# Five edits to a one-core backward kernel: product shapes, weight transposes, gradient stores, small matmul widths, early weight chunks

## The chip, the cores and the metric

The kernel is written for one core of a Trainium2 chip. That core has a matrix engine (PE, with a weight load PEld in front of each matmul), a vector engine (DVE), an activation engine (ACT), GpSimd (POOL) and a queue engine (SP). Each of them carries out its own instructions strictly in their written order. DMAs are issued by SP, ACT and POOL. The metric is the device time of one execution in microseconds (us), lower is better.

## What is computed

The reference is one gated block and its gradients. With L = 2048, D = 576, N = 128 and F = 4608:

```
xn  = layernorm(x)
s   = causal_conv(xn, K) + xn * Dskip                   # K from A, B, C, dt: D x L
g   = silu( (silu(xn @ w1) * (xn @ w3)) @ w2 )
out = x + s * g
returns out and the gradients of x, A_re, A_im, B_re, B_im, C_re, C_im,
        log_dt, Dskip, w1, w3, w2
```

All matmul inputs are bf16. The convolution is done by blocks of 512 with transforms written as matmuls. The gradients of A, B, C and log_dt need, for each of the 576 channels, sums over time of a gradient times powers of the rates; the kernel gets them as products of two small factors ("q" over 64 steps, "pz" over 32), in 36 chunks of 16 channels.

## The kernel before

The program is unrolled in Python, and a planner orders it: `self.at(us)` sets a planned time as the priority of what is written next, and the planner turns the priorities, the data dependences and its own estimates into one fixed order for every engine and queue. Buffers come from pools; a tile that is asked for again waits for its last user. Planned times and times of the trace are not the same: T0 = 560 of `backward` corresponds to about 800 us in the trace, T2 = 1208 to about 1610 us.

The stages, in order of time in the trace:

- **Prologue (0 to 150).** Layer norm, selectors, spectra of the input.
- **Hidden layer beside the convolution kernel (150 to 530).** `ffn_hidden` makes gate and up for every 512 of F; pairs of row tiles go to DRAM (`GI_dram`, L728, from POOL; `gu_t` has three buffers) and the product to `H_dram` (L727, from SP). `kgen_chunk` makes q and pz for the 36 chunks; `pz` is stored in three planes (minus cosine, cosine, sine; the first is made by POOL in L477).
- **`forward_tail` (530 to 800).** w2 is loaded in nine chunks of 4 x 128 rows (`w2g`, L769, from POOL), then the second layer, the convolution and the gradient of the gate branch; `go_o` is transposed by PE (L833) into `goT`.
- **`ssm_bwd_conv` and 18 groups of 256 columns of F (800 to 1605).** A group (`phase6_group`) makes the hidden gradient (`ph`, L1226), copies it (`gh`, L1229, ACT), multiplies it into `gu` and `gg` (L1232, DVE), stores both to `GU_dram` and `GG_dram` in halves (L1239, from SP), and makes the weight gradients (L1254, L1273, L1279, L1281). ACT evicts each of these and issues the DMA that stores it (L1259, L1276, L1285, L1286). `load_w2T` brings the group's w2 rows (two POOL loads, two transposing DMAs on SP), and `gates` prepares the next group from two loads of `GI_dram` on POOL (L1193, L1194).
- **`param_chunk` (19 chunks from about 1300 on, 17 in the last stage).** SP loads `gz`, `qT` (a transposing DMA) and `pz`. For each half of a chunk PE makes two PSUM tiles of 8 channels x 2 x 32 (`et_ps`, L989; the pool has three buffers). DVE multiplies each with two planes of pz (four instructions, L996, into `pr_q`) and sums (two, L998). Five `final_block`s turn the sums into gradients: DVE works in two scratch tiles `f0` and `f1` (L1029), ACT copies results out of them (L1050) and after each copy issues the DMA that stores it (L1051).
- **`phase6_inputs` (1605 to the end).** For 16 row tiles, the gradient of xn: `ggc` and `guc` are transposed from DRAM by SP (two buffers each), and 144 matmuls per tile (L1333) use w1 and w3 transposed. These come in four parts, through `wT_into` (L1131): `wTA` (12 of 36 column blocks, own memory), `wTB` (12), `goT`'s memory (4) and `go_o`'s memory (8). Each part is five transposing DMAs for w1 and five for w3, one for every 128 rows of D (the last has 64).

All DMA transposes are issued by line L1140, on SP.

Of the kernel before, what the change touches and what calls it, by code (L numbers as in the profile page):

```python
# [11 lines left out]
ALU = mybir.AluOpType  # L12
# [4 lines left out]
P = 128  # L17
# [43 lines left out]
class K:  # L61
# [356 lines left out]
    def ssm_kernel(self, T0, TK):  # L418
# [9 lines left out]
        PS = bass.MemoryType.PSUM  # L428
        self.PZ_dram = self.dram.tile([P, NCH, 3, DC, AV], BF16, name="PZ_dram")
        self.Q_dram = self.dram.tile([NCH, P, 2 * DC * BV], BF16, name="Q_dram")  # L430
# [24 lines left out]
    def kgen_chunk(self, ch, E, lhs, mp, sb, qvp, ps, T, TK):  # L455
# [14 lines left out]
        q = qvp.tile([P, DC, 2, BV], BF16, name="q_k")  # L470
        pz = sb.tile([P, 3, DC, AV], BF16, name="pz_k")
        for k, src in ((1, S), (0, C)):
            tt(out=q[:, :, k, :], in0=E[:, 0:QW].rearrange("p (d b) -> p d b", b=BV),
               in1=src[:, 0:QW].rearrange("p (d b) -> p d b", b=BV), op=ALU.mult)
            tt(out=pz[:, 1 + k].rearrange("p d a -> p (d a)"), in0=E[:, QW:], in1=src[:, QW:], op=ALU.mult)
        nc.sync.dma_start(out=self.Q_dram[ch], in_=q[:].rearrange("p d k b -> p (d k b)"))
        nc.gpsimd.tensor_scalar(out=pz[:, 0], in0=pz[:, 2], scalar1=-1.0, scalar2=None, op0=ALU.mult)  # L477
        nc.sync.dma_start(out=self.PZ_dram[:, ch], in_=pz[:])
        v = qvp.tile([P, 2, DC, AV], BF16, name="v_k")
        for k, (Wa, Wb, op) in enumerate(((self.WrT, self.nWiT, ALU.add), (self.nWiT, self.WrT, ALU.subtract))):  # L480
            t = sb.tile([P, DC, AV], BF16, name="t_k")
            for r, W, o in ((1, Wb, t[:]), (0, Wa, v[:, k])):
                tt(out=o.rearrange("p d (a x) -> p d a x", x=4),
                   in0=pz[:, 1 + r].rearrange("p d (a x) -> p d a x", x=4),
                   in1=W[:, ch].rearrange("p h d x -> p (h d) x")[:, :, None, :].to_broadcast([P, DC, AV // 4, 4]),
                   op=ALU.mult)
            tt(out=v[:, k], in0=v[:, k], in1=t[:], op=op)
# [243 lines left out]
    def forward_tail(self, T0, TB, TQ, gctx):  # L731
# [20 lines left out]
        ep = rpool(fw, "o_ep", 2)  # L752
        ep1 = rpool(fw, "o_ep1", 1)
        wpool = rpool(fw, "o_w", 1)
        hp = rpool(fw, "o_h", 2)
# [7 lines left out]
        for t_ in self.goT:  # L763
            nc.gpsimd.memset(t_[rem:P, nfull, :], 0.0)
        w2g = [wpool.tile([P, GRP, D], BF16, name=f"w2g{n}") for n in range(FT // GRP)]
        w2 = [w2g[fi // GRP][:, fi % GRP, :] for fi in range(FT)]
        for n, t_ in enumerate(w2g):
            self.at(T0 - 4 + 2.5 * n)
            nc.gpsimd.dma_start(out=t_[:], in_=aps["B_w2"][n * GRP * P:(n + 1) * GRP * P, :].rearrange(  # L769
                "(c p) d -> p c d", p=P))  # L770
# [46 lines left out]
        for t_ in self.goT[NB // 2:]:  # L817
            nc.gpsimd.memset(t_[rem:P, nfull, :], 0.0)
        self.w2rows = [rowp.tile([P, DT * P], BF16, name=f"w2r{i}") for i in range(4)]
        for w2r in self.w2rows:  # L820
            nc.gpsimd.memset(w2r[:, D:DT * P], 0.0)
        out0 = aps["out_0"].flatten_outer_dims()
        xin = aps["A_u"].flatten_outer_dims()
        for i in range(LT):
# [6 lines left out]
            ptr = tps.tile([P, 1024], BF16, name="ptr")  # L831
            for c, (do, dsz) in enumerate(cfg.dch):
                nc.tensor.transpose(ptr[0:dsz, c * P:(c + 1) * P], go_o[:, i, do:do + dsz], self.ident_bf[:])  # L833
            ts = slice(i % KT * P, (i % KT + 1) * P)
            nc.scalar.copy(out=self.goT[m][:, 0:nfull, ts],
                           in_=ptr[:, 0:nfull * P].rearrange("p (c t) -> p c t", t=P))
            nc.vector.tensor_copy(out=self.goT[m][0:rem, nfull, ts], in_=ptr[0:rem, nfull * P:(nfull + 1) * P])
            self.at(T0 + 44 + TB * i)
# [9 lines left out]
    def ssm_bwd_conv(self, T0, TQ, ps):  # L848
# [3 lines left out]
        with self.tc.tile_pool(name="b_k", bufs=1, side="right") as kp, self.tc.tile_pool(name="b_z", bufs=2, side="right") as zp:  # L852
# [4 lines left out]
            nc.vector.tensor_scalar(out=self.lcol[:], in0=self.lcol[:], scalar1=1.0 / 512, scalar2=None, op0=ALU.mult)  # L857
            self.ones_col = kp.tile([P, 1], BF16, name="ones_col")
            nc.vector.memset(self.ones_col[:], 1.0)
# [3 lines left out]
    def ssm_bwd_params(self, chunk_at, final_at, out, big, S_all, ps):  # L863
# [4 lines left out]
        with self.tc.tile_pool(name="g_k", bufs=1, side="right") as gkp, self.tc.tile_pool(name="g_t", bufs=3, side="right") as tqp, \  # L868
                self.tc.tile_pool(name="g_q", bufs=2, side="right") as qp, \
                self.tc.tile_pool(name="g_r", bufs=1, side="right") as rp:  # L870
            gz = []
            for i in range(2):
# [13 lines left out]
    def conv_bwd_quarter(self, g, kp, zp, ps, T0, TQ):  # L886
# [22 lines left out]
        for b in range(NB):  # L909
# [6 lines left out]
            for tt in range(KT):  # L916
                nc.tensor.matmul(gds[0:1, 0:W], lhsT=self.ones_col[:], rhs=prod[:, tt, :], start=(b == 0 and tt == 0),
                                 stop=(b == NB - 1 and tt == KT - 1))
# [51 lines left out]
    def param_chunk(self, ch, gz, S_all, tqp, qp, rp, ps):  # L970
# [3 lines left out]
        if True:  # L974
# [7 lines left out]
            pz = qp.tile([P, 3, 16, AV], BF16, name="pz")  # L982
            nc.sync.dma_start(out=pz[:], in_=self.PZ_dram[:, ch])
            for h in range(2):
                T = [ps.tile([P, 8, 2, AV], FP32, name="et_ps") for _ in range(2)]
                for dd in range(8):
                    dl = 2 * dd + h
                    for r in range(2):
                        nc.tensor.matmul(T[r][:, dd].rearrange("p k (f t) -> p (k f) t", f=2), lhsT=qT[:, dl, :],  # L989
                                         rhs=gK[:, r, :, :, dl, :].rearrange("p k f t -> p (k f) t"),  # L990
                                         start=True, stop=True)
                d0 = h * (D // 2) + ch * 8
                for s in range(2):
                    pr = rp.tile([P, 2, 8, 2, AV], FP32, name="pr_q")
                    for r in range(2):
                        nc.vector.tensor_tensor(out=pr[:, r], in0=T[r][:], in1=pz[:, s + r, h * 8:h * 8 + 8, :][:, :, None, :]  # L996
                                                .to_broadcast([P, 8, 2, AV]), op=ALU.mult)
                    nc.vector.tensor_reduce(out=S_all[:, 2 * s:2 * s + 2, d0:d0 + 8].rearrange("p k d -> p d k"),  # L998
                                            in_=pr[:].rearrange("p r d k a -> p d k r a"), op=ALU.add, axis=AX.XY)

# [9 lines left out]
    def final_block(self, c, do, dsz, fp, fo, S_all, ps2):  # L1010
# [17 lines left out]
        S2 = ST[v].rearrange("p (r s) n -> p s r n", s=2)[:, 1]  # L1028
        A, B = [fp.tile([P, 4, N], FP32, name=f"f{n}")[v] for n in range(2)]  # L1029
        acc = fp.tile([P, 4], FP32, name="acc")[v]  # L1030
# [48 lines left out]
    def backward(self, T0, TG, TQ, TX, gctx, mats):  # L1079
# [11 lines left out]
        with ExitStack() as out:  # L1091
# [13 lines left out]
            for ai in range(2):  # L1105
                t = wA.tile([P, FA, D], BF16, name=f"wTA{ai}")
                self.wT_into(t[:], ai, 0, wT, lambda c: T2 - 160 + 12 * (2 * c + ai))
            T1 = T0 + 4 * TQ
            N1 = 19
            chunk_at = lambda ch: T1 + 13.5 * ch if ch < N1 else T2 + TX * 1.4 + 13.5 * (ch - N1)  # L1110
            final_at = {20: {0: T2 + 4.5 * TX}, 30: {3: chunk_at(30) + 10}, 33: {1: chunk_at(33) + 10},
# [19 lines left out]
    def wT_into(self, dst, ai, f0, wT, at):  # L1131
        n = dst.shape[1]
        for c, (do, dsz) in enumerate(self.cfg.dch):
            self.at(at(c))
            self.nat_transpose(dst[:, :, do:do + dsz], self.aps[("B_w1", "B_w3")[ai]][do:do + dsz, f0 * P:(f0 + n) * P])
        for f in range(n):
            wT[ai][f0 + f] = dst[:, f, :]
# [6 lines left out]
    def load_w2T(self, gi, T):  # L1144
        nc, cfg = self.nc, self.cfg
        nfl = self.FG // P
        self.at(T)
        w2T = self.wp.tile([P, nfl, cfg.DT, P], BF16, name="w2T")
        for fl in range(nfl):
            fi = gi * nfl + fl  # L1150
            w2r = self.w2rows[fi % len(self.w2rows)]
            nc.gpsimd.dma_start(out=w2r[:, 0:cfg.D], in_=self.aps["B_w2"][fi * P:(fi + 1) * P, :])
            self.nat_transpose(w2T[:, fl], w2r[:])
        return w2T
# [56 lines left out]
    def phase6_group(self, gi, tiles, gwp, ps_h, ps_gw, defer):  # L1211
# [5 lines left out]
        for s in range(LH // 2):  # L1217
# [13 lines left out]
            for t_ in (gu, gg):  # L1231
                nc.vector.tensor_tensor(out=t_[:, sl], in0=gh.rearrange("p j t f -> p (j t) f"), in1=t_[:, sl],  # L1232
                                        op=ALU.mult)
            if s % 2 == 1 and not defer:
                self.phase6_grad2(gi, s // 2, hn, ps_gw, "pgw")
        for (dst, t_) in ((self.GU_dram, gu), (self.GG_dram, gg)):
            for j in range(2):
                ts = slice(j * LH, (j + 1) * LH)
                nc.sync.dma_start(out=dst[ts, :, gi * FG:(gi + 1) * FG].rearrange("t p f -> p t f"), in_=t_[:, ts, :])  # L1239
        self.phase6_grad13(gi, gg, gu, gwp, ps_gw)  # L1240
# [47 lines left out]
    def phase6_inputs(self, T2, TX, FA, wT, late, ps_gw, ps_h, ffps):  # L1288
# [6 lines left out]
        with self.tc.tile_pool(name="x_in", bufs=2) as inp, self.tc.tile_pool(name="x_wB", bufs=1) as wB, \  # L1295
# [10 lines left out]
            def weights(tiles, f0, t):  # L1306
                for ai in range(2):
                    self.wT_into(tiles[ai], ai, f0, wT, lambda c: t)
                return f0 + tiles[0].shape[1]
# [169 lines left out]
```

## Time and profile before

| | us |
|---|---|
| four runs | 2022.34, 2010.83, 2008.61, 2011.96; median 2011.39 |
| the profiled execution (the first of the four) | 2022.34 |
| its span, first to last instruction | 2020.4 |
| PE matmul busy | 1772.6 (88%) |
| PE weight loads | 1297.8 (64%) |
| DVE | 1419.7 (70%) |
| ACT | 1024.2 (51%) |
| POOL | 269.6 (13%) |

The profile's page gives busy time per engine, 40 slices of the span, the DMA queues, the chain of waits that ended last, the costliest groups of instructions and the DMA issues. A group's row reads: line, engine, operation, output <- inputs, shapes, count | busy time, mean ns of one | idle time of the engine just before, and what ended it. The mean granted PE clock over the span is 0.958 of full speed.

### The profile page before, as it was taken

The numbers are of one execution on the slowest core, as the hardware profiler recorded it, in microseconds if no ns is written. First come the engines' busy times: TensorE is split into PE (matmuls) and PEld (weight loads), VectorE is DVE, ScalarE is ACT, GpSimd is POOL, SyncE is SP. The second block draws the span as 40 slices with busy tenths as digits, with TensorE's granted clock in tenths as the row PEclk, the third lists the DMA queues.
The fourth block names the chain that finished last, engine by engine and source line by source line (L and its number), as shares of the span: only waits on it lengthen the run. The fifth ranks groups of instructions, "written<-read, shape, count | busy, mean of one in ns | idle before, by whom it ended". The sixth has DMA issues, their size and how long they took to land. (4 is left out here: it accounts for less than half of the span.)

```text
span 2020.4 us, 41956 instructions
## 1 busy us (share of the span) xinstructions
PE 1772.6 (88%) x17179; PEld 1297.8 (64%) x17179; DVE 1419.7 (70%) x2660; ACT 1024.2 (51%) x1739; POOL 269.6 (13%) x362
## 2 busy tenths in 40 slices
PE   2789999999799988989889998879979967988787
PEld 1444444444478866778777777768768845766666
DVE  7538888888387743495884868758979804398676
ACT  2778888887545554774666656434445201100112
POOL 4003333333321221000000000100000000000000
PEclk9899999999899999999999999989999978999999
DMA  3589888797966688365563555899998999999992
GB/s 85 181 298 320 299 298 297 271 328 274 273 190 157 161 228 222 104 181 159 176 189 115 170 172 151 216 234 235 236 186 212 221 194 186 198 198 196 205 187 56
DMA packets 612907, 417.10 MB, mean 206 GB/s; under 512 B 400395, under 2 KB 558059, under 8 KB 607979
## 3 DMA queue, kind: packets, MB, share of 16 engines
q1 hardware_dynamic: 547200, 280.47, 56.8%
q0 software_dynamic: 24288, 106.94, 15.5%
q10 hardware_dynamic: 41226, 27.02, 5.3%
q8 instruction: 134, 2.20, 0.5%
q14 instruction: 59, 0.48, 0.1%
HBM read 134.06 MB, written 188.01 MB: 159 GB/s over the span
## 5 line engine op out<-in xcount | busy, mean ns | idle before, releaser
L719 PE MATMUL pgu<-wmB_w,xnT 128*128 128x512 bf16 x1152 | 282.4, 380 | 1.2 <-ACT E_k L392 1.2
L1273 PEld LDWEIGHTS <-xn_bf 128*128 128x128 bf16 x2304 | 223.9, 98 | 29.4 <-issue 2.6
L1273 PE MATMUL pgw<-Y,xn_bf 128*128 128x256 bf16 x2048 | 232.3, 273 | 1.6 <-ACT gw L1275 1.6
L996 DVE TENSOR_TENSOR pr_q<-et_ps,pz 128x512 f32<-128x512 f32 x288 | 186.2, 683 | 46.9 <-PE et_ps L989 37.3
L1226 PE MATMUL ph<-w2T,goT 128*128 128x256 bf16 x1440 | 193.3, 283 | 23.3 <-ACT gh L1229 23.2
L719 PEld LDWEIGHTS <-xnT 128*128 128x128 bf16 x1152 | 103.2, 98 | 124.0 <-issue 18.9
L998 DVE TENSOR_REDUCE S_all<-pr_q 128x16 f32<-128x1024 f32 x144 | 175.2, 1216 | 2.2
L1226 PEld LDWEIGHTS <-goT 128*128 128x128 bf16 x1440 | 142.2, 102 | 35.0 <-issue 13.8
L1232 DVE TENSOR_TENSOR Y<-gh,Y 128x1024 bf16<-128x1024 bf16 x128 | 86.3, 682 | 110.8 <-ACT gh L1229 109.3
L785 PE MATMUL po<-w2g,hc 128*128 128x288 bf16 x1152 | 154.1, 292 | 4.2 <-DMA hc<-H_dram 4.2
L1275 ACT CAST gw<-pgw 128x256 bf16<-128x256 f32 x144 | 54.0, 377 | 198.5 <-PE pgw L1273 195.7
L1333 PEld LDWEIGHTS <-ggc 128*128 128x128 bf16 x1152 | 114.8, 101 | 51.8 <-issue 9.5
L1333 PEld LDWEIGHTS <-guc 128*128 128x128 bf16 x1152 | 115.1, 101 | 51.2 <-DMA guc<-GU_dram 18.7
L785 PEld LDWEIGHTS <-hc 128*128 128x128 bf16 x1152 | 113.1, 100 | 34.1 <-DMA hc<-H_dram 4.5
L1373 ACT ACTIVATE X<-X 128x576 f32<-128x576 f32 x16 | 10.9, 683 | 224.0 <-DVE X L1343 205.5
L1254 PE MATMUL pgw<-go_o,X 128*128 128x288 bf16 x896 | 120.2, 288 | 0.0
L722 ACT ACTIVATE s_t<-pgu 128x512 bf16<-128x512 f32 x144 | 87.3, 608 | 52.2 <-PE pgu L721 51.9
L1229 ACT CAST gh<-ph 128x512 bf16<-128x512 f32 x144 | 84.2, 616 | 55.3 <-PE ph L1226 37.5
L1254 PEld LDWEIGHTS <-X 128*128 128x128 bf16 x960 | 93.5, 98 | 23.6 <-issue 0.6
L989 PE MATMUL et_ps<-gz,qT 128*128 128x64 bf16 x1152 | 57.6, 198 | 46.7 <-DVE pr_q L996 39.9
L582 PEld LDWEIGHTS <-dSi 128*128 128x128 bf16 x768 | 76.2, 100 | 34.8 <-issue 33.8
L724 ACT CAST gu_t<-pgu 128x1024 bf16<-128x1024 f32 x90 | 91.9, 1021 | 12.5 <-DMA GI_dram<-gu_t 12.5
(328 smaller groups left out, 3986.3 us busy)
## 6 DMA issues: line engine op xcount, KB each, us to landing
GI_dram<-gu_t POOLq DMA_DIRECT2D x72, 512.0 KB, 5.7
Y<-GI_dram POOLq DMA_DIRECT2D x19, 1024.0 KB, 7.1
H_dram<-h_t SPq DMA_DIRECT2D x72, 256.0 KB, 5.2
Q_dram<-q_k SPq DMA_DIRECT2D x36, 512.0 KB, 5.1
X<-GI_dram POOLq DMA_DIRECT2D x18, 1024.0 KB, 7.8
GU_dram<-Y SPq DMA_DIRECT2D x34, 512.0 KB, 4.9
GG_dram<-Y SPq DMA_DIRECT2D x30, 512.0 KB, 4.9
E_dram<-E_k SPq DMA_DIRECT2D x18, 768.0 KB, 3.8
```

Source lines behind the costliest of these rows:

```text
L719: nc.tensor.matmul(pgu[:, j], lhsT=xnT[:, c, ts], rhs=wm[w][:, c, :], start=(c == 0), stop=False)
L722: nc.scalar.activation(out=s_t[:, :, q, :], in_=pgu[:, 0].rearrange("p (g f) -> p g f", g=ng), func=ACT.Silu)
L724: cp(out=gu_t[:, :, :, q, :], in_=pgu[:].rearrange("p u (g f) -> p u g f", g=ng))
L785: nc.tensor.matmul(pos[k][:, pi_, 0:pw], lhsT=hcs[k][:, fi, :], rhs=w2[fi][:, po:po + pw], start=(fi == 0), stop=(fi == FT - 1))
L996: nc.vector.tensor_tensor(out=pr[:, r], in0=T[r][:], in1=pz[:, s + r, h * 8:h * 8 + 8, :][:, :, None, :] .to_broadcast([P, 8, 2, AV]), op= ...
L998: nc.vector.tensor_reduce(out=S_all[:, 2 * s:2 * s + 2, d0:d0 + 8].rearrange("p k d -> p d k"), in_=pr[:].rearrange("p r d k a -> p d k r ...
L1226: nc.tensor.matmul(ph[j][:, k, :].rearrange("p (a f) -> p a f", f=P), lhsT=lw, rhs=rh, start=(n == 0), stop=(n == nfull))
L1229: nc.scalar.copy(out=gh[:, j], in_=ph[j])
L1232: nc.vector.tensor_tensor(out=t_[:, sl], in0=gh.rearrange("p j t f -> p (j t) f"), in1=t_[:, sl], op=ALU.mult)
L1254: nc.tensor.matmul(pgw[pi_][:, 0:pw], lhsT=hn[:, tt, fl * P:(fl + 1) * P], rhs=go_o[:, tt, po:po + pw], start=(tt == 0), stop=(tt == LT - 1))
L1273: nc.tensor.matmul(pw_[:, 0:FG], lhsT=self.xn_bf[:, tt, c * P:(c + 1) * P], rhs=nat[:, tt, :], start=(tt == 0), stop=(tt == LT - 1))
L1333: nc.tensor.matmul(px[pi_][:, 0:pw], lhsT=act[:, fi, :], rhs=wT[ai][fi][:, po:po + pw], start=(fi == 0 and ai == 0), stop=(fi == FT - 1 an ...
```

## The change

**Products.** `pz` is stored in two planes; `param_chunk` makes the negative plane itself with one DVE instruction on loading. PSUM tiles are laid out [2, 8, 32] instead of [8, 2, 32], so that one DVE instruction multiplies a tile with two planes, and one reduction serves both. `pr_q` doubles to 8 KB per partition. The scratch tiles of `final_block` no longer have memory of their own: they are the one buffer of `pr_q`.

```
-                T = [ps.tile([P, 8, 2, AV], FP32, name="et_ps") for _ in range(2)]
+            nc.sync.dma_start(out=pz[:, 1:3], in_=self.PZ_dram[:, ch])
+            nc.vector.tensor_scalar(out=pz[:, 0], in0=pz[:, 2], scalar1=-1.0, scalar2=None, op0=ALU.mult)
+                T = [ps.tile([P, 2, 8, AV], FP32, name="et_ps") for _ in range(2)]
...
-                for s in range(2):
-                    pr = rp.tile([P, 2, 8, 2, AV], FP32, name="pr_q")
-                    for r in range(2):
-                        nc.vector.tensor_tensor(out=pr[:, r], in0=T[r][:], in1=pz[:, s + r, ...])
-                    nc.vector.tensor_reduce(out=S_all[:, 2 * s:2 * s + 2, d0:d0 + 8]...)
+                pr = rp.tile([P, 2, 4, 8, AV], FP32, name="pr_q")
+                for r in range(2):
+                    nc.vector.tensor_tensor(out=pr[:, r]..., in0=T[r][:]..., in1=pz[:, r:r + 2, ...]...)
+                nc.vector.tensor_reduce(out=S_all[:, :, d0:d0 + 8], in_=pr[:]..., axis=AX.XY)
...
-        A, B = [fp.tile([P, 4, N], FP32, name=f"f{n}")[v] for n in range(2)]
+        ws = self.rp.tile([P, 2, 4, 8, cfg.AV], FP32, name="pr_q")[v].rearrange("p r k d a -> p (r k d a)")
+        A, B = [ws[:, n * 4 * N:(n + 1) * 4 * N].rearrange("p (k n) -> p k n", n=N) for n in range(2)]
...
-            chunk_at = lambda ch: T1 + 13.5 * ch if ch < N1 else ...
+            chunk_at = lambda ch: T1 + 12 + 13 * ch if ch < N1 else ...
```

**Weight transposes.** `wT_into` issues one transposing DMA over all 576 rows instead of five, `load_w2T` one load and one transpose instead of two of each, and the two `wTA` parts are planned later.

```
-                self.wT_into(t[:], ai, 0, wT, lambda c: T2 - 160 + 12 * (2 * c + ai))
+                self.wT_into(t[:], ai, 0, wT, T2 - 90 + 36 * ai)
...
-        for c, (do, dsz) in enumerate(self.cfg.dch):
-            self.at(at(c))
-            self.nat_transpose(dst[:, :, do:do + dsz], ...[do:do + dsz, f0 * P:(f0 + n) * P])
+        self.at(at)
+        self.nat_transpose(dst, self.aps[("B_w1", "B_w3")[ai]][:, f0 * P:(f0 + n) * P])
...
-            nc.gpsimd.dma_start(out=w2r[:, 0:cfg.D], ...)
-            self.nat_transpose(w2T[:, fl], w2r[:])
+        nc.gpsimd.dma_start(out=w2r[:, :, 0:cfg.D], ...)
+        self.nat_transpose(w2T[:].rearrange("p l c f -> p (l c) f"), w2r[:].rearrange("p l d -> p (l d)"))
```

**Gradient stores.** The stores to `GU_dram` and `GG_dram` go from SP to POOL, written after each half instead of after the group's loop.

```
+            if s % 2 == 1:
+                ts = slice(s // 2 * LH, (s // 2 + 1) * LH)
+                for (dst, t_) in ((self.GU_dram, gu), (self.GG_dram, gg)):
+                    nc.gpsimd.dma_start(out=dst[ts, :, ...], in_=t_[:, ts, :])
...
-        for (dst, t_) in ((self.GU_dram, gu), (self.GG_dram, gg)):
-            for j in range(2):
-                nc.sync.dma_start(out=dst[ts, :, ...], in_=t_[:, ts, :])
```

**Small matmuls.** The fifth PE transpose of each `go_o` tile takes the last 128 columns instead of the last 64, and DVE copies the upper half of the result. `ones_col` becomes 128 x 128, so that L917 fills 128 rows of PSUM, of which the first is used.

**Early chunks of w2.** The first two `w2g` chunks are in a pool of their own and are planned 60 us earlier.

```
+        wpoolE = rpool(fw, "o_wE", 1)
...
-        w2g = [wpool.tile([P, GRP, D], BF16, name=f"w2g{n}") for n in range(FT // GRP)]
+        w2g = [(wpoolE if n < 2 else wpool).tile([P, GRP, D], BF16, name=f"w2g{n}") for n in range(FT // GRP)]
...
-            self.at(T0 - 4 + 2.5 * n)
+            self.at(T0 - 4 + 2.5 * n - (60 if n < 2 else 0))
```

## The prediction

> **What bounds the kernel now.** I read three views, in this order: busy time by stage, the PE's waits, and queue by queue the timelines around PE's long idle stretches. First the stages (stretch, length, then busy us of PE, PEld, DVE, ACT, POOL, the granted clock, the DMA share, GB/s):
>
> ```profile
> 150.00:530.00 380.00, 377.27 (x3787) 166.61 (x3786) 316.00 (x585) 310.62 (x367) 127.56 (x117) 1.00 0.86 294
> 1300.00:1350.00 50.00, 34.86 (x356) 29.39 (x354) 23.35 (x35) 13.27 (x25) 5.68 (x6) 0.90 1.10 242
> 1350.00:1605.00 255.00, 236.57 (x2518) 201.42 (x2519) 227.01 (x311) 120.97 (x198) 8.56 (x16) 0.97 0.92 215
> 1605.00:1692.00 87.00, 58.56 (x481) 44.10 (x475) 24.81 (x38) 6.96 (x18) 0.00 (x0) 0.84 1.00 202
> 1692.00:2020.00 328.00, 281.78 (x2527) 217.81 (x2527) 220.68 (x420) 40.51 (x96) 12.62 (x24) 0.94 0.94 175
> ```
>
> PE is the bound wherever it is full: from 150 to 530 it idles 2.7 of 380 us, so nothing that the change does to DVE, POOL or DMA there counts. Idle PE is 15 us in 1300:1350, 18 in 1350:1605, 28 in 1605:1692 and 46 in 1692:2020. The clock below 1.00 says that idling also slows what follows. The waits of PE (total, times, longest) name the stretches:
>
> ```profile
> PE et_ps L989 <- DVE pr_q L996: 39.9, 24, 9.3
> PE ph L1226 <- ACT gh L1229: 23.2, 12, 11.5
> PE et_ps L626 <- ACT gu_t L724: 13.5, 1, 13.5
> PE px L1333 <- DMA wTB<-in_B_w_dram: 8.6, 2, 8.2
> ```
>
> **1. Early w2 chunks: -4.5 us.** The 13.5 us wait is at 530.9. PE has no PSUM before ACT has evicted the last hidden tiles, and ACT waits for a `gu_t` buffer:
>
> ```profile
> 517.95 3.75 POOL L769 DMA_DIRECT2D w2g<-in_B_w_dram  x5 [3.14 <-PE pgu L721]
> 521.68 0.91 POOL L728 DMA_DIRECT2D GI_dram<-gu_t  x1
> 541.92 1.01 ACT L724 CAST gu_t<-pgu 128x1024 bf16<-128x1024 f32 x1 [12.52 <-DMA GI_dram<-gu_t]
> ```
>
> The store issued at 521.68 frees the buffer, but it stands on POOL's queue behind five w2 chunks of 576 KB. Two of the five go. By the semaphores the chunks land 1.8 us apart (533.4 to 540.3): 2 x 1.8 = 3.6 us sooner. By the average since 517.95, 3392 KB in 24 us, two chunks are 8.2 us. I take 4.5, nearer to the landings, as the first one was 15 us late whatever came behind it. The two early loads lie among stores that land in a median of 5.7 us with three buffers; if they delayed one so far that ACT waits, the whole gain could go (bounds 0 and -8.2).
>
> **2. Later wTA: -11.5 us.** The 11.5 us wait for `gh` is at 1338.9. ACT was not working:
>
> ```profile
> 1342.92 0.49 ACTq L1285 DMA_DIRECT2D out_dram<-gwt  x1
> 1349.17 0.47 ACTq L1286 DMA_DIRECT2D out_dram<-gwt  x1
> 1349.74 1.07 ACT L1229 CAST gh<-ph 128x512 bf16<-128x512 f32 x2 [12.87 <-DMA wTA<-in_B_w_dram]
> ```
>
> ACT stood at its own two DMA issues. In the trace's operands the DMAs of SP and ACT take turns over eight semaphores, and an issue waits until the DMA eight places before it has landed. The semaphore of L1286 is that of a wTA transpose that landed at 1349.15. So seven small transposes in a row (first row of the next fence) take nearly all the turns, and a 32 KB store waits for them. After the change a wTA part is one turn, not five, and lies where no conv work ends. I remove the 11.5 us and 2 us of slow clock behind it, and give 2 us back for two transposes of some 8 us on SP near 1500 and 1545, in front of `qT`, `gz` and `pz`, for which DVE's products wait (-15.4 with the 3.9 us gap at 1305.9; 0 if ACT meets the long transposes there).
>
> **3. Single transposes at the start of the last stage: -8 us.** From 1612 to 1669 the chain of waits is nothing but SP issuing transposes:
>
> ```profile
> 1335.50 17.11 SPq L1140 DMA_TRANSPOSE wTA<-in_B_w_dram  x7
> ...
> 1623.49 20.11 SPq L1140 DMA_TRANSPOSE wTB<-in_B_w_dram  x10
> 1643.65 6.40 SPq L1140 DMA_TRANSPOSE ggc<-GG_dram  x2
> ...
> 1655.99 14.30 SPq L1140 DMA_TRANSPOSE go_o<-in_B_w_dram  x10
> ```
>
> The pieces of `go_o` have a median of 1307 ns, those of `goT`, half as large, 1218: a small transpose costs an issue, not its bytes. A large one costs bytes: the 34-block piece of `ggc` (1.11 MB) took 5.67 and 5.11 us. At 5.4 us, a single `go_o` load of 1.18 MB is 5.7, two are 11.5 (-2.8), and the two `wTB` of 1.77 MB are 17.2 (-2.9). That is -5.7, and 2.3 more because PE's 8.2 us wait for wTB becomes short enough not to slow the clock (after it, pairs of L1333 came 0.48 us apart, later 0.25). The Trainium skill, page "DMA: Bandwidth & Descriptors", section "Latency and other measured facts", gives DMA transposes 261 GB/s with a non-contiguous middle dimension and some 350 to 400 when contiguous; a single load writes 576 contiguous elements instead of 128. By that, 5.9 MB would take 15.7 us instead of 34.4: -18.7. But `ggc` writes contiguously already, and its 1.11 MB in 5.4 us are 206 GB/s. I take the row; bounds -2 and -19. The `goT` loads and wTA lie beside PE work: nothing.
>
> **4. Gradient stores on POOL: -2 us.** 72 stores leave SP and the eight turns; SP stood 1 to 5 us at some. Against it speaks the skill, page "SBUF — State Buffer", section "SBUF: two separate sides": GpSimd cannot write DMA descriptors while DVE holds the shared port in a two-port mode. In the trace POOL's stores (L728) take 0.97 us each and land in a median of 5.7 us, beside a busy DVE, against 5.3 for SP's (L1239): 0.4 us a store, off the path, where the rule would add up to one DVE instruction each. I take the row. Behind a waiting store on POOL stand the next group's w2 rows and GI loads, and for these ACT's `gates`, which already waited 23.2 us for them, with PE's `ph` behind. Half a us for each of 18 groups is +9; the remaining 11.7 us of PE's waits for `gh`, were half of them SP's doing, are -6.
>
> **5. Wide products: -4 us.** The two rows (count | busy, mean ns):
>
> ```profile
> L996 DVE TENSOR_TENSOR pr_q<-et_ps,pz 128x512 f32<-128x512 f32 x288 | 186.2, 683 | 46.9 <-PE et_ps L989 37.3
> L998 DVE TENSOR_REDUCE S_all<-pr_q 128x16 f32<-128x1024 f32 x144 | 175.2, 1216 | 2.2
> ```
>
> 512 more elements cost 533 ns, so 1.04 ns each and 150 ns fixed. A half chunk now is 4 x 683 + 2 x 1216 = 5164 ns, then 2 x 1216 + 2282 = 4714: 72 x 0.45 = 32 us less, less 36 negations at about 0.28 us (a bf16 copy of 576 took 0.30): 22 us of DVE. On the path is only what PE waits for products alone: 39.9 less the four long stretches (9.3, 6.2, 7.9, 8.0), which have other causes, is 8.5. DVE is 89% busy in 1350:1605, and a PSUM tile is released after one instruction instead of three. I take half; bounds 0 and -15.
>
> **6. One buffer for products and finals: +6 us.** After the change no product can start from a final's first DVE instruction until ACT's last copy of it, and ACT again stands at its stores, behind `guc`'s turns:
>
> ```profile
> 1916.45 0.42 DVE L1034 TENSOR_TENSOR f<-rates 128x256 f32<-128x256 bf16 x1 [14.14 <-ACT gout L1050]
> ```
>
> This happens already, as the next final is written early into `f0`: DVE stood 5.9, 14.1 and 9.6 us after three finals, and PE lost 6.2, 7.9 and 8.0. These 22 us stay. New is that the 12.7 us of products that DVE did inside the three holds (17, 28 and 20 us long) come after them. PE fills three PSUM buffers and then matmuls of a row tile, so I take half; bounds -10 (the hoisted finals were planned badly) and +30.
>
> **Nothing:** the negation on POOL (36 x 1.49 us) and a third of pz's store lie under a full PE; the wider transpose and `ones_col` keep 219 and 224 ns, as a matmul's row counts the moving columns. `chunk_at` ends 3 planned us later; `load_w2T` is prefetched a group ahead.
>
> **Sum:** -4.5 - 11.5 - 8 - 2 - 4 + 6 = -24. Against the profiled execution's 2022.3 that is 1998. The other three runs lie 10 to 14 us below it, and it has one stretch in which all DMAs landed late (a GI load issued at 1481.3 took 18.2 us, median 7.8) and PE idled 9.3; I count that as its own and take the 24 from the median: 1987.
>
> **Rivals.** *Moved, not removed:* ACT meets the two long wTA transposes near 1500 in the same way, and single loads go at the old rate; left are 1, 4 and 5 less 6: -4.5, so 2007. For it: the DMA share is 0.92 to 1.10 there. Against: one turn of eight. *The shared buffer decides:* holds of 65.7 us plus 9 of new leads stop PE throughout: 75 - 22 = +53, with the other gains (-30) 2034. It decides once the holds cost PE some 30 us more than now. Against: PE has 17 us of row-tile matmuls to put between. *More than I take:* contiguous transposes at the page's rate (-19), the hoisted finals gone (-10), the 3.9 us gap with wTA, w2 at -8: about 1958. That an edit does nothing holds for the small widths.
>
> **Chances.** Forecast (1973 to 2001) 0.52, more 0.20, moved 0.14, shared buffer 0.14. What a measurement can tell from no change is about 0.5%, 10 us: faster 0.73, same 0.13, slower 0.14. The range leaves out a third of "more" and half or more of "shared buffer": 1962 to 2016.
>
> **What would show it.** Right: the gap before L626 is under 10 us and before L1226 near 1338 gone; SP's stretch for wTB and `go_o` is near 29 us; L996 near 1.22 us x144, L998 near 2.28 x72. Wrong: PE waits for `pr_q` of over 60 us after finals; ACT standing at stores near 1500 behind wTA; GI loads landing later behind POOL's stores.

## The result and the profile after

The changed kernel takes 2023.9 us (median of 43 runs, 2001.6 to 2055.1), the kernel before 2017.0 (64 runs, 1995.7 to 2039.3). The ratio is 1.0036, interval 1.0016 to 1.0057: 3 to 11 us longer, where 24 us less were forecast. Medians here are of all executions, while ratios leave out those more than 1.5% above the fastest of their kernel, so the two can differ by a few thousandths. The profiled execution took 2040.6 us (span 2038.8), 17 above its median, so a second trace (after_again, 2016.4 us, 7 below its median) stands beside it.

The PE's waits (total, times, longest), for the four rows shown of before:

```profile
PE et_ps L992 <- DVE pr_q L998: 58.4, 25, 8.0
...
PE pgw L1278 <- ACT gw L1280: 20.1, 3, 18.7
...
PE ph L1230 <- ACT gh L1233: 12.2, 12, 1.9
...
PE et_ps L625 <- ACT gu_t L723: 7.2, 1, 7.2
PE px L1338 <- DMA wTB<-in_B_w_dram: 6.6, 2, 4.8
```

Three rows fell: `ph` by 11.0, L625 by 6.3, wTB by 2.0; the first two not for the reason forecast, as shown below. The products' row rose by 18.5 to 58.4, and a wait of 18.7 us has appeared on a weight gradient (`pgw`, 1326 to 1345). Before, DVE hardly waited for `pz`, and at a product:

```profile
DVE pr_q L996 <- DMA pz<-PZ_dram: 5.6, 2, 4.6
```

Now its list of waits begins with a row that the kernel before doesn't have:

```profile
DVE pz L986 <- DMA pz<-PZ_dram: 137.7, 21, 29.5
```

L986 is the negation. Its row in the groups, below the two that were to become wide:

```profile
L998 DVE TENSOR_TENSOR pr_q<-et_ps,pz 128x1024 f32<-128x1024 f32 x144 | 170.5, 1217 | 50.6 <-PE et_ps L992 39.2
...
L1003 DVE TENSOR_REDUCE S_all<-pr_q 128x32 f32<-128x2048 f32 x72 | 164.2, 2281 | 0.9
...
L986 DVE TENSOR_SCALAR pz<-pz 128x512 bf16<-128x512 bf16 x36 | 10.7, 298 | 137.8 <-DMA pz<-PZ_dram 137.7
```

The durations are near those of the forecast (1216, 2282 and about 280 ns). What it left out stands behind the second bar: 137.8 us of idle DVE. How that reaches PE is seen in the timelines of DVE and PE (start, length, work, idle time before it):

```profile
1426.23 0.68 DVE L1212 TENSOR_TENSOR Y<-Y,X 128x1024 bf16<-128x1024 bf16 x1
1432.97 0.29 DVE L986 TENSOR_SCALAR pz<-pz 128x512 bf16<-128x512 bf16 x1 [6.06 <-DMA pz<-PZ_dram]
1433.18 0.68 DVE L1213 TENSOR_TENSOR X<-Y,X 128x1024 bf16<-128x1024 bf16 x1
1433.78 1.22 DVE L998 TENSOR_TENSOR pr_q<-et_ps,pz 128x1024 f32<-128x1024 f32 x1
1435.03 2.29 DVE L1003 TENSOR_REDUCE S_all<-pr_q 128x32 f32<-128x2048 f32 x1
```

```profile
1427.67 0.87 PE L992 MATMUL et_ps<-gz,qT 128*128 128x64 bf16 x24
...
1435.05 0.59 PE L992 MATMUL et_ps<-gz,qT 128*128 128x64 bf16 x8 [5.74 <-DVE pr_q L998]
```

The negation for the next chunk stands in DVE's order ahead of the current chunk's second product. It waits 6 us for a load; the product behind it, whose PSUM tile PE had filled by 1428.5 (24 matmuls, all three buffers), waits with it, and PE, which needs that tile again, is idle from 1429.3 to 1435.1.

The order of SP and ACT at the end of the conv stage (timeline) shows what became of the wTA transposes:

```profile
1299.02 7.24 SPq L1145 DMA_TRANSPOSE wTA<-in_B_w_dram  x1
...
1307.19 10.95 SPq L1145 DMA_TRANSPOSE wTA<-in_B_w_dram  x1
...
1319.49 7.12 SPq L1145 DMA_TRANSPOSE qT<-Q_dram  x1
1326.66 0.60 SPq L985 DMA_DIRECT2D pz<-PZ_dram  x1
...
1343.64 0.39 ACTq L1281 DMA_DIRECT2D out_dram<-gw  x1
...
1344.36 0.65 ACT L1280 CAST gw<-pgw 128x256 bf16<-128x256 f32 x2 [21.39 <-DMA pz<-PZ_dram]
```

They aren't late at all. Both stand at 1299 to 1318, ahead of the first chunk's loads, so the first chunk starts at 1352 instead of 1310 (1345 in the second trace). And ACT stands at a store in the same way as before: L1281's semaphore is that of the `pz` load of 1326.66, which landed at 1343.56.

The stages, cut at each kernel's own marks (group stage: last transpose of `go_o` to last `ph`; last stage: from there to the end), in the columns of the forecast's first fence:

```profile
800.00:1651.00 851.00, 742.98 (x7665) 636.61 (x7663) 611.17 (x1013) 444.52 (x934) 99.29 (x127) 0.96 0.72 179
1651.00:2039.00 388.00, 324.01 (x2861) 252.27 (x2857) 237.11 (x369) 45.26 (x108) 12.65 (x24) 0.91 0.85 178
```

Before, these were 825 and 401 us. The last stage became 13 shorter, the group stage 26 longer with the same 743 us of PE in it. But in the second trace the stages are 817 and 392 us, with 805 us ahead of them where the kernel before has 794. So a longer group stage belongs to the one long execution, and the two traces don't show where a median execution loses its 7 us.

### The profile page after: what moved, and what is told of

It is laid out like the page before. It is cut to its first block, busy times and chain, and to the rows that moved or that the text cites. A ratio compares the mean times of both kernels' runs of the same rounds, so it can differ in the third digit from the quotient of the medians.

```text
span 2038.8 us, 41560 instructions
## 1 busy us (share of the span) xinstructions
PE 1772.1 (87%) x17179; PEld 1304.9 (64%) x17179; DVE 1404.3 (69%) x2480; ACT 1023.4 (50%) x1739; POOL 270.4 (13%) x378
## 4 chain that ended last, share of the span: by engine, by line
PE 39%; DVE 20%; DMA 16%; ACT 13%; issue 5%; SPq 4%; POOL 1%; ACTq 0%; DVEq 0%; POOLq 0%
PE pgu L718 7%; PE pgw L1278 7%; DMA pz<-PZ_dram 5%; DVE pr_q L998 4%; PE pgw L1338 4%; PE px L1338 4%; SPq L1145 3%; PE po L785 3%; DVE S_all L1003 3%; PE pgw L1259 2%; PE ph L1230 2%; PE kps L499 2%; ACT gk_st L948 2%; PE et_ps L581 2%; DMA gs<-GS_dram 2%
## 5 line engine op out<-in xcount | busy, mean ns | idle before, releaser
L1278 PE MATMUL pgw<-Y,xn_bf 128*128 128x256 bf16 x2048 | 234.2, 274 | 20.4 <-ACT gw L1280 20.1
L998 DVE TENSOR_TENSOR pr_q<-et_ps,pz 128x1024 f32<-128x1024 f32 x144 | 170.5, 1217 | 50.6 <-PE et_ps L992 39.2
L1003 DVE TENSOR_REDUCE S_all<-pr_q 128x32 f32<-128x2048 f32 x72 | 164.2, 2281 | 0.9
L785 PEld LDWEIGHTS <-hc 128*128 128x128 bf16 x1152 | 113.5, 100 | 33.7 <-DMA hc<-H_dram 4.8
L992 PE MATMUL et_ps<-gz,qT 128*128 128x64 bf16 x1152 | 56.0, 198 | 59.4 <-DVE pr_q L998 58.4
L727 POOL DMA_DIRECT2D GI_dram<-gu_t x72 | 65.3, 907 | 305.5 <-DVE gu_t L723 210.5
L986 DVE TENSOR_SCALAR pz<-pz 128x512 bf16<-128x512 bf16 x36 | 10.7, 298 | 137.8 <-DMA pz<-PZ_dram 137.7
```

What stands on the lines that cost most here:

```text
L727: nc.gpsimd.dma_start(out=self.GI_dram[fb * ng:(fb + 1) * ng, :, :, i0:i0 + NT, :].rearrange("g p u t f -> p u g (t f)"), in_=gu_t[:].rear ...
L785: nc.tensor.matmul(pos[k][:, pi_, 0:pw], lhsT=hcs[k][:, fi, :], rhs=w2[fi][:, po:po + pw], start=(fi == 0), stop=(fi == FT - 1))
L998: nc.vector.tensor_tensor(out=pr[:, r].rearrange("p (s k) d a -> p s k (d a)", s=2), in0=T[r][:].rearrange("p k d a -> p k (d a)")[:, None ...
L1003: nc.vector.tensor_reduce(out=S_all[:, :, d0:d0 + 8], in_=pr[:].rearrange("p r k d a -> p k d r a"), op=ALU.add, axis=AX.XY)
L1278: nc.tensor.matmul(pw_[:, 0:FG], lhsT=self.xn_bf[:, tt, c * P:(c + 1) * P], rhs=nat[:, tt, :], start=(tt == 0), stop=(tt == LT - 1))
```

## The experiments

Each ratio is to the kernel before, run on the same chip. "Late" counts the stretches between 1270 and the last `ph` in which DMAs took over 13 us from issue to landing; group and last stage are lengths in us in the one profiled execution. Runs on one chip: after_again, no_neg, wta_dep, neg_dep; before_neg, nd_sp, nd_w2late, nd_pieces; neg_dep_b, nd_sp_b, gg_sp, before_pool; nd_w2T2, before_pool_w2T, nd_sp_narrow, nd_sp_w2late; nd_narrow, noneg_sp. Two kernels ran on two chips each, and their ratios differ by 0.004 (neg_dep, neg_dep_b) and 0.006 (nd_sp, nd_sp_b): 7 and 12 us. A smaller difference between chips says nothing.

| | ratio, interval | group | last | late |
|---|---|---|---|---|
| before | 1 | 825 | 401 | 1 |
| before_neg | 1.0276, 1.0225 to 1.0327 | 855 | 412 | 1 |
| before_pool | 0.9979, 0.9952 to 1.0006 | 810 | 396 | 0 |
| before_pool_w2T | 0.9975, 0.9941 to 1.0009 | 813 | 392 | 0 |
| changed kernel | 1.0036, 1.0016 to 1.0057 | 851 | 388 | 4 |
| after_again | 1.0064, 1.0035 to 1.0093 | 817 | 392 | 4 |
| wta_dep | 1.0039, 1.0011 to 1.0067 | 837 | 394 | 5 |
| gg_sp | 0.9983, 0.9952 to 1.0013 | 822 | 381 | 1 |
| no_neg | 0.9898, 0.9846 to 0.9950 | 845 | 371 | 6 |
| neg_dep | 0.9830, 0.9786 to 0.9873 | 833 | 373 | 4 |
| neg_dep_b | 0.9867, 0.9834 to 0.9899 | 833 | 375 | 5 |
| nd_w2late | 0.9929, 0.9900 to 0.9959 | 822 | 367 | 3 |
| nd_w2T2 | 0.9895, 0.9853 to 0.9938 | 827 | 369 | 4 |
| nd_pieces | 1.0045, 1.0015 to 1.0075 | 834 | 376 | 4 |
| nd_narrow | 0.9864, 0.9816 to 0.9912 | 800 | 394 | 1 |
| nd_sp | 0.9839, 0.9785 to 0.9892 | 800 | 369 | 1 |
| nd_sp_b | 0.9777, 0.9718 to 0.9837 | 807 | 366 | 1 |
| nd_sp_w2late | 0.9764, 0.9721 to 0.9808 | 802 | 366 | 1 |
| nd_sp_narrow | 0.9814, 0.9768 to 0.9859 | 793 | 378 | 1 |
| noneg_sp | 0.9802, 0.9763 to 0.9841 | 807 | 375 | 1 |

**The changed kernel again.**

> The changed kernel once more, for a second trace of it. Three theories of where the forecast 24 us went. Negation theory: DVE's new negation of pz stands in DVE's order ahead of products whose data are there, so DVE waits some 138 us for pz loads and PE some 30 us more at pr_q; in this trace the wait of DVE for pz is again over 100 us. Transpose theory: the two long wTA transposes lie at the end of the conv stage, in front of the first chunks' loads; the first chunk's matmuls again start about 40 us later than before (1352 against 1310) and PE again has one gap of 10 to 20 us near 1330. Contention theory: both are accidents of one execution with slow DMAs and are absent or halved here. Ratio to the kernel before by all three: 1.00 to 1.006.

DVE's wait for `pz` was 88.6 us, PE's for `pr_q` 40.2, its gap near 1330 5.2, the first chunk at 1345. The late start comes back and the sizes don't: the wait for `pz` stayed under the 100 expected, PE's wait for the products is no longer than before (39.9), and of the 18.7 us gap 5.2 are left.

**Without the negation on DVE.** The planes are stored as before.

```
-        self.PZ_dram = self.dram.tile([P, NCH, 2, DC, AV], BF16, name="PZ_dram")
+        self.PZ_dram = self.dram.tile([P, NCH, 3, DC, AV], BF16, name="PZ_dram")
...
+        nc.gpsimd.tensor_scalar(out=pz[:, 0], in0=pz[:, 2], scalar1=-1.0, scalar2=None, op0=ALU.mult)
...
-            nc.sync.dma_start(out=pz[:, 1:3], in_=self.PZ_dram[:, ch])
-            nc.vector.tensor_scalar(out=pz[:, 0], in0=pz[:, 2], scalar1=-1.0, scalar2=None, op0=ALU.mult)
+            nc.sync.dma_start(out=pz[:], in_=self.PZ_dram[:, ch])
```

> The changed kernel with the three planes of pz stored in DRAM as before (negation back on POOL while the planes are made), wide products and all else kept. Negation theory: DVE's wait for pz falls from 138 us to under 50, the PE's wait for pr_q from 58 to about 40, time 10 to 20 us below the changed kernel. Transpose theory: the first chunk still starts near 1350 and the time stays within 5 us of the changed kernel. Contention theory: no change, or slower by a few us as pz's loads are half as large again.

```profile
DVE pr_q L998 <- DMA pz<-PZ_dram: 25.5, 2, 24.9
...
PE et_ps L992 <- DVE pr_q L998: 26.1, 26, 12.7
```

1988.2 us, against 2023.9 of its neighbour after_again: 1.0064 to 0.9898, some 33 us, more than the negation theory asked. DVE waits 25.5 us for `pz` instead of 137.7 or 88.6 (the two traces of the changed kernel), PE 26.1 for `pr_q` instead of 58.4 or 40.2. The first chunk still starts at 1330.

**The negation alone, in the kernel before** (the same lines, the other way round):

> The kernel before with one edit of the change alone: pz in two planes, and the negative plane made by one DVE instruction when it is loaded. Negation theory: DVE waits for pz for 80 us or more where it waited 6, PE's wait for pr_q rises from 40 to 55 or more, and the time rises by 15 to 35 us (ratio 1.008 to 1.017). Rival, that the negation only hurts together with the wide products and their shared buffer: ratio within 0.997 to 1.003.

```profile
PE et_ps L989 <- DVE pr_q L996: 88.7, 28, 8.4
```

Ratio 1.0276: 55 us for 36 instructions of 0.29 us, 10.5 us of work. PE's wait for the products went from 39.9 to 88.7, DVE's for `pz` from 5.6 to 130.4. The negation needs neither the wide products nor the shared buffer to hurt. The edit also plans the program anew: up to some 180 of DVE's 2660 other instructions stand at another place in its order (40 of 2444 between the changed kernel and no_neg), so the price is that of the negation with the order that came with it.

**wTA really late, alone and with the three planes.** The two transposes follow a one-element copy of a sum of chunk 10 and of chunk 13.

```
+                if ch in self.late_wA:
+                    ai, wA_t, wT = self.late_wA[ch]
+                    self.nc.vector.tensor_copy(out=wA_t[ai][0:1, 0, 0:1], in_=S_all[0:1, 0, ...])
+                    self.wT_into(wA_t[ai][:], ai, 0, wT, chunk_at(ch) + 13)
```

> The changed kernel with the two wTA transposes really put late: each follows a one-element DVE copy of a sum of chunk 10 and of chunk 13, so they can't be taken at the end of the conv stage. Transpose theory: the first chunk starts near 1315 instead of 1352, the gap near 1330 is under 6 us, the time falls by 12 to 30 us, unless ACT meets the transposes near 1500. Negation theory: the first chunk starts earlier, but DVE still waits over 100 us for pz and PE over 50 for pr_q, and the time falls by less than 8 us. Contention theory: within 5 us of the changed kernel.

> Both edits together: planes of pz stored in three as before, and wTA put behind chunks 10 and 13. If both theories hold and are independent, the gains add: 25 to 40 us below the changed kernel, so near 1985 to 1995. If one of them holds alone, the time is that of the single edit within 6 us. Contention theory: within 8 us of the changed kernel.

In wta_dep the first chunk starts at 1300 (ten matmuls; the next at 1318) and the gap near 1330 is gone, but the time is only 0.0025 below after_again, with overlapping intervals: the start was worth little while DVE waited (114.3 us for `pz`). With both edits 1981.4, or 0.983; the second run gave 0.9867. Since no_neg alone had 0.9898, wTA's place is worth some 6 to 14 us at most, and the intervals overlap.

The late place has a gap of its own. In neg_dep (timelines):

```profile
1484.69 28.70 SPq L1151 DMA_TRANSPOSE wTA<-in_B_w_dram  x1
...
1515.68 2.72 PE L1236 MATMUL ph<-w2T,goT 128*128 128x256 bf16 x12 [16.50 <-ACT gh L1239]
```

The transpose holds SP 28.7 us instead of some 8, a GI load beside it lands late, ACT waits for that load 20.8 us, and PE for ACT's `gh`. Of the eleven traces with late wTA seven have this gap near 1500 (6.9 to 16.5 us); the five with early single transposes have 5.2 to 18.7 us between 1310 and 1361.

**The gradient stores: POOL against SP.** The edit puts the stores back behind the loop (`nc.sync.dma_start` over both halves). nd_sp and nd_sp_b are neg_dep with it, gg_sp is the changed kernel with it, before_pool the kernel before with the stores on POOL.

> The kernel with three stored planes and late wTA (neg_dep), and the gradient stores of the groups back on SP, written after the loop. If POOL's stores are what makes DMAs land late (five such stretches in 1300 to 1620 there, one before), there are two or fewer such stretches and the time falls by 8 to 25 us. If they are worth what the prediction said (-2), it rises by 0 to 5 us. If they keep ACT's and SP's turns free and that matters more, it rises by over 8 us.

> neg_dep once more, as the partner of nd_sp_b on one chip: ratio to before 0.979 to 0.988 as in its first run; in the group stage (1300 to 1620) at least three stretches in which DMAs take over 13 us to land.

> neg_dep with the gradient stores on SP, beside its partner. Store theory (POOL's stores among SP's transposes make all DMAs land late, some 15 us of PE each time): one or two such stretches, 10 to 30 us below neg_dep_b. Prediction's step 4 (POOL's stores gain 2 us): 0 to 5 us above neg_dep_b. If the single look at 1959 was luck: equal within 6 us.

> The changed kernel with the gradient stores on SP and nothing else undone. Store theory: fewer late stretches in the group stage (one or two instead of three to five) and 8 to 25 us less than the changed kernel (ratio 0.992 to 1.001 to before), unless DVE's waits for pz, which stay, already cover them. Prediction's step 4: 2 us more than the changed kernel (ratio 1.006).

> The kernel before with the gradient stores on POOL after each half, nothing else of the change. Store theory: three or more late stretches in the group stage instead of one, 10 to 30 us slower than before (ratio 1.005 to 1.015). Prediction's step 4: 2 us faster, bounds -6 to +9 (ratio 0.997 to 1.0045).

Side by side, neg_dep_b has 0.9867 and nd_sp_b 0.9777 (1983.0 and 1967.4 us); gg_sp lies at 0.9983 where the changed kernel has 1.0036 to 1.0064. Yet in the kernel before the same stores on POOL cost nothing (0.9979): there the forecast of -2 us lies in the interval and the store theory fails. The column of late stretches says where: 3 to 6 in all nine kernels that have wide products and POOL's stores, none or one in the eleven that lack either. Such a stretch in no_neg (timeline, then the window of PE's gap):

```profile
1408.73 5.16 SPq L1145 DMA_TRANSPOSE qT<-Q_dram  x1
1408.93 0.57 POOL L1197 DMA_DIRECT2D Y<-GI_dram  x1 [14.87 <-PE et_ps L992]
...
1430.06 1.06 ACT L1208 ACTIVATE Y<-Y 128x1024 bf16<-128x1024 bf16 x1 [20.19 <-DMA Y<-GI_dram]
...
1431.64 0.58 PE L1230 MATMUL ph<-w2T,goT 128*128 128x256 bf16 x2 [15.88 <-ACT gh L1233]
```

```profile
1415.00:1432.00 17.00, 1.12 (x9) 0.78 (x8) 0.85 (x1) 1.94 (x4) 0.00 (x0) 0.61 0.99 103
```

A 1 MB load takes 21.1 us instead of its median of 6.3. ACT waits for it with the next group's gates; `gh`, behind them in ACT's order, comes late, and PE with it. The DMA engines are full (0.99) and move 103 GB/s. In nd_sp_b the group stage has one such stretch (at 1471, with the wTA transpose). Its two stages:

```profile
795.00:1602.00 807.00, 736.36 (x7658) 632.07 (x7656) 605.73 (x994) 444.47 (x934) 33.91 (x54) 0.98 0.72 192
1602.00:1968.00 366.00, 315.60 (x2864) 246.69 (x2860) 233.66 (x354) 45.39 (x108) 12.63 (x24) 0.95 0.92 195
```

Against the second trace of the changed kernel (817 and 392 us, clock 0.98 and 0.91) the group stage is 10 us shorter and the last stage 26, at a clock of 0.95, with 9 us less of PE's own work in it. nd_sp_b also lacks the negation on DVE, so this isn't the stores' doing alone.

**What POOL's stores collide with.** nd_w2T2 is neg_dep with two loads and two transposes of w2 for each group, before_pool_w2T is before_pool with single ones; nd_narrow is neg_dep with the products of before and finals in `f0` and `f1`.

> neg_dep (stores on POOL) with w2's rows of a group in two loads and two transposes again. If the long w2 transposes beside POOL's stores make the late stretches, they fall to one or two and the time by 8 to 18 us (ratio 0.977 to 0.983). If the pairing doesn't matter: ratio 0.983 to 0.989, three or more late stretches.

> The kernel before with the stores on POOL and single w2 loads and transposes. If the pair of edits makes the cost: ratio 1.003 to 1.012 and three or more late stretches. If not: ratio 0.995 to 1.001 as with the stores alone.

> neg_dep (stores on POOL) with the narrow products of before and finals in their own memory. If the wide products are what POOL's stores collide with: ratio 0.975 to 0.983, as with the stores on SP (nd_sp_narrow 0.981), and two or fewer late stretches. If not: 0.984 to 0.995 and three or more.

The pairing of w2 is ruled out from both sides. In nd_narrow the late stretches go (one left) and the group stage takes 800 us. Its time, 0.9864, still missed what was expected. In the traces its last stage took 394 us where nd_sp_narrow has 378; nothing that POOL stores lies there, and this stays open.

**Terms of the sum, taken out one by one.** nd_w2late and nd_sp_w2late put the two w2 chunks back into `wpool`, at the old time; nd_pieces cuts the last stage's weight loads into five; nd_sp_narrow has the products and finals of before; noneg_sp is nd_sp with wTA where the changed kernel has it.

> neg_dep with all nine w2 chunks late, as before. Prediction's step 1: 4.5 us slower. If the gain is given back right behind it, since the H transposes start earlier into the remaining chunks and land later (gap near 564), then from 700 on the stage lies where it lay, and the time is within 2 us.

> neg_dep with the last stage's weight transposes (wTB, goT, go_o) in five pieces again, wTA and w2T single. Prediction's step 3: SP's stretch for wTB and go_o rises from some 27 to some 34 us and the time by 6 to 8 us, all of it between the first and the third row tile of the last stage. Rival, that SP's stretch isn't what the stage waits for: within 2 us.

> nd_sp with all w2 chunks late. Step 1 of the prediction: 4.5 us slower than nd_sp. If the chunks don't matter: within 3 us of nd_sp (ratio 0.978 to 0.984), the gap in front of L626 between 10 and 20 us with and without them.

> nd_sp with the narrow products of before (four multiplies and two sums for each half) and finals in memory of their own. Steps 5 and 6 of the prediction together (-4 and +6): 2 us faster than nd_sp. If the wide products free PE's tiles and the shared buffer costs nothing: 8 to 25 us slower, most of it in the last stage (some 343 us there).

> nd_sp without the late wTA: the two single wTA transposes stand where the planner puts them, at the end of the conv stage. Prediction's step 2 (11.5 us for taking wTA away from there): ratio 0.984 to 0.990, a gap of 8 us or more near 1310 to 1340. If the place of wTA doesn't matter once the stores are on SP: 0.977 to 0.983.

With the stores on SP, none of these edits moves the time beyond the intervals of nd_sp and nd_sp_b (0.984 and 0.978): 0.976 without early chunks, 0.981 with narrow products, 0.980 with wTA early. With the stores on POOL the same kind of edit, against the two runs of neg_dep, moved it by 0.006 to 0.021: nd_w2late to 0.993, nd_pieces to 1.0045. The order of all other instructions on DVE, ACT, POOL and SP is the same as in neg_dep, but both ran on another chip than neg_dep's two, and what a chip adds is not excluded. For nd_pieces SP's stretch grew as expected, from 15.56 + 9.80 to 17.94 + 14.07 us (+6.7), and the last stage from 373 or 375 to 376, but the median of the runs by some 30 us more than that. Both profiled executions of neg_dep lie 19 and 28 us above their medians, so the traces don't show where; how many late stretches an execution meets is a plausible place, and not shown.

nd_sp_w2late (1965.3 us, 0.9764) and nd_sp_b (0.9777) are shorter than both kernels of this study. Not tried: the same negation placed behind the products of the current chunk, which would part its place from its work; a third `pz` buffer; and wide products with finals in memory of their own.

## Why the prediction was wrong

The step that failed is one clause of step 5: "less 36 negations at about 0.28 us (a bf16 copy of 576 took 0.30): 22 us of DVE". It priced the added instruction by its own length and not by its wait. On an engine that works in order, an instruction that waits for a DMA is a gate for all that is behind it; before, the first product of a chunk waited for `pz` itself, and by then PE's tiles were there and `pz` mostly too (5.6 us in all). Four pairs price the negation: 1.0064 to 0.9898, 1.0039 to 0.983, 0.9983 to 0.9802, and 1.0276 to 1 (the third pair on two chips): 33 to 55 us.

The way through the products is seen, but it isn't all of it. PE's wait for them differs by 49 us in before_neg (of 55), and in the other pairs by 14 (after_again, no_neg; of 33), 36 (wta_dep, neg_dep; of 42) and 8 (gg_sp, noneg_sp; of 36). Where the rest goes the traces don't show.

- **Step 1, early chunks (-4.5): 0 with the stores on SP.** With them on POOL, late chunks were 0.006 to 0.010 slower, which stays open (other chip, as said). The chunks were issued at 137, not some 60 us before the others at 520. The gap at L625 fell to 7.2, the sign that I had named, but not by the chunks: that was luck. It is 3.9 to 7.2 us in the five kernels without POOL's negation (7.0 in before_neg, which has the chunks late), and 8.5 to 22.2 in the fifteen that have it (early chunks in nd_sp 14.6, in nd_sp_b 18.0, late ones in nd_sp_w2late 21.5). The edit that I put under "Nothing" because PE was full had freed POOL's queue. And it was given back: the DMAs issued from 541 on landed late. The transposes of H held SP 20.5 us instead of 8.3, a GI store took 20.1 us, POOL stood behind it, and PE, which needed POOL's `k` through DVE, stood 8.1 us at 559 (16.5 at 563 in the second trace, for a load of `cu`). From the last hidden tile to the last `go_o` transpose it is 267 us, before 263.
- **Step 2, later wTA (-11.5): the move did not happen.** The planned time is a priority, and I read it as a date: the planner put the transposes at 1299, ahead of the first chunk's loads, which were planned earlier (that it takes whatever is ready first is argued). The 11.5 us gap at `gh` was gone, as I had named for a sign, and stood 18.7 us long at `pgw` instead. Forced late, they are worth 0 with the stores on SP and 6 to 14 us at most with them on POOL. The rival "moved, not removed" is what the traces show: PE stood 16.5 us near 1500 in neg_dep and 12.4 in nd_sp_b.
- **Step 3, single transposes (-8):** right on SP, 17.17 + 10.06 = 27.2 us instead of 34.4, and the row of `ggc` was the better guide than the page's rate, which asked for 15.7. PE's wait for wTB is 6.6 us, 2.0 less. What this is worth in time stays open, since nd_pieces was 36 to 43 us slower for 6.7 us of SP.
- **Step 4, stores on POOL (-2):** right in the kernel before, wrong beside the wide products. Four pairs with wide products differ by 11 to 33 us in SP's favour (neg_dep_b, no_neg, nd_w2late and the changed kernel, each with its partner); a fifth, neg_dep and nd_sp, doesn't differ. Only the first, 18 us, ran on one chip. The narrow pair, nd_narrow and nd_sp_narrow, differs by 10 us with overlapping intervals. I had weighed the rule of the Trainium skill's page "SBUF — State Buffer", section "SBUF: two separate sides", against rows of a trace with narrow products, so the rows could not speak for the kernel to come. But the rule can't either: by the same section `tensor_tensor` has no two-port mode, `tensor_reduce` never contends on trn2, and outside those modes an instruction with at most one SBUF input doesn't contend with GpSimd. The products read one tile from PSUM and one from SBUF, so by the page neither width should hold POOL up. The median landing of `GG_dram` stores from 1290 to 1640 doesn't decide it: 6.7 to 9.9 us in the nine kernels with wide products and POOL's stores, 7.6 in nd_narrow, 6.2 and 6.6 in before_pool and before_pool_w2T, 5.2 from SP in nd_sp_b. Why width and POOL's stores go badly together stays open.
- **Steps 5 and 6, wide products and the shared buffer (-4 + 6):** taken out together on SP's side, 0 within the interval. DVE waited for ACT's copies in finals no longer than before (9.6 us, in no_neg 21.8, before 33.7); the rival "shared buffer decides" is out. The wait for `pr_q` that I had named as its sign came to 58.4 us (40.2 in the second trace), from the negation.

The sum itself is nearly met where the negation is gone, 0.9898 or 20 us less in no_neg against the 24 forecast, but by a chance of the terms: in its trace the last stage is 30 us shorter than before, and the group stage, with six late stretches, 20 longer. (The rival "more" comes to 1953, not 1958, if step 6 counts -10 as its bounds say.)

## What to carry to other kernels

Price an added instruction by what it waits for and what stands behind it on its engine, before its length: 10 us of DVE work cost 33 to 55. Look up in the built order where a moved DMA really stands, and then whether its stall was removed or only moved: a wTA transpose came with a gap of PE at the early place and mostly at the late one too. And weigh a rule against rows only when these rows have the shapes that the change brings: POOL's stores were free in the kernel before, and beside wide products cost 11 us or more in four pairs of five.

## What the hardware showed unexpectedly

In the stretches of 13 to 38 us counted above, one to six DMAs land late while the DMA engines are full. They aren't alike. In no_neg's gap they move 103 GB/s at a share of 0.99 and PE stands, against 215 at 0.92 in 1350:1605 of the kernel before. In nd_w2T2, where a `qT` transpose, both stores, a `w2r` and a GI load are late between 1429 and 1454, they move 198, and PE works 22.9 of 24.1 us. So a late stretch costs only where PE needs what is late. In about half of them (20 of the 39 in the nine kernels) a transposing DMA is itself among the late ones. Between 1270 and the last `ph` they are common (3 to 6 in a trace instead of none or one) only with wide products and stores on POOL. That pair isn't the only way to them: from 531 to 585, before any product or gradient store, nine DMAs of gg_sp land late, one after 44.6 us, and between 548 and 577 the engines move 116 GB/s at a share of 1.12. What goes on inside the DMA engines no run here shows.
